# Four lasting two-bank PSUM buffers, used whole or by one bank, and a newly searched instruction order in a recurrence and FFN kernel

## The chip, the cores and the metric

The kernel runs on one NeuronCore of one Trainium2 chip. The metric is the device time of one execution in microseconds, from the median of the runs. The engines are TensorE (PE in the profile), VectorE (DVE), ScalarE (ACT), GpSimd (POOL) and SyncE (SP), which here only issues DMAs. PSUM, TensorE's output memory, has eight banks of 2 KB per partition.

## The reference

Two stages. First a linear-attention recurrence over 768 steps for 4 x 8 heads of width 40, then a feed-forward network on its 3072 rows of 320:

```python
for t in range(S):
    y[:, :, t] = np.einsum('bhd,bhde->bhe', rt, state)
    Sa = np.einsum('bhde,bhe->bhd', state, at)
    state_decay = state * wt[:, :, None, :] - np.einsum('bhd,bhe->bhde', Sa, bt)
    state = state_decay + np.einsum('bhd,bhe->bhde', vt, kt)
...
h = x @ w_in          # 320 -> 2048
r = np.maximum(h, 0.0)
return ((r * r) @ w_out).astype(np.float32)   # 2048 -> 320
```

Inputs and output are float32; the matmuls run on bfloat16.

## The kernel before, in words

**Chunks.** Time is cut into 12 chunks of 64 steps (c = 0 to 11). For each chunk the kernel loads r, k, v, w, a, b, prepares them (`prep`, `keys`, `keys_by8`), advances the state (`rec`), reads the result (`read`) and runs the feed-forward network on the chunk's 256 rows (`ffn`). Chunks 0 to 3 (BY8) use another layout of loads and keys than the later ones.

**The operations by name.** Each operation in the order has a short name with its chunk, and a suffix for its part:

- loads `ldw`, `ldk`, `ldb`, `lda`, `ldr`, `ldv` on SP; the weights come as `lwi`, `lwl`, `lwo`; the casts are `cast…`, `cwi`, `cwl`, `cwo`; the logarithms of the decays are `ln`, split into `hi` and `lo`
- sums of the decays on TensorE, `ci` and `cf`, and their exponentials on ScalarE: `eg`, `ef`, `ec`, `ei`, `ex` (lines 542, 603, 620, 626, 653)
- transposes on TensorE, `TA`, `TR`, `TK`, `TV`, `TU`, `TS`, `Tb`, `Tk`, `XT`, each followed by a copy or product out of PSUM under the same name with a small t. For the names in WIDE a transpose is done whole (128 x 128 blocks over the whole array, line 387), otherwise in pieces on half of the array (line 383)
- the two triangular products `EN` and `CX` in two halves g0 and g1, masked on VectorE by `mEN` and `mCX` (line 704)
- the recurrence: `AS`, `EV`, `u0`, `NU`, `u1` (VU), then `SC`, `S`, and `s`, which writes the state (line 796); the read-out is `RS`, `Y`, `y`, `yd`, `XT`, `xt`
- the first product of the network in four parts u0 to u3, each of eight matmuls `F` and four `FL` for the last 64 features on half of the array (line 893); then ReLU `f` (lines 921, 923) and square `q` (lines 927, 929, 931)
- the second product `O` in four parts (line 379): eight matmuls each, alternating between the two token halves, which lie in the two banks of one buffer. One copy `o` of 640 columns brings both halves out, one store `st` writes them. Only in the last chunk the halves are apart: `OL … g0` and `OL … g1` have a buffer each, of which one bank is used, and a copy `oe` each.

**The order.** Nothing is scheduled at run time or by the framework. A search outside the kernel wrote the text ORDER: entry after entry names the engine and the operation, and `Plan.issue` emits them in that order, so each engine's queue follows the text. A number behind PE is the PSUM buffer that the operation takes. Entries `W…` are filler matmuls that TensorE runs while it would wait (line 1044). Dependences between engines become semaphore waits when the program is built.

**PSUM.** There are four names pb0 to pb3, each two banks wide. Every operation that takes a buffer gets a new tile under that name (`slot`, and `fill` at line 1038), and waits until the readers of the one before are done.

Of the kernel before, what the change touches and what calls it, by code (L numbers as in the profile page):

```python
# [82 lines left out]
SP ldb 0; PE1 cf 0 h0; ACT castk 0; ACT ln 0 h1; SP lda 0; POOL castb 0; SP ldw 1; SP ldb 1; PE2 Tk
0; DVE hi 0 h1; DVE lo 0 h1; SP ldv 0; PE cf 0 h1; ACT eg 0; POOL castA 0; PE3 WD1; PE3 Tb 0; PE ci
0 h1; DVE tb 0 g0; SP ldk 1; ACT ef 0; ACT ln 1; SP ldr 0; SP lda 1; POOL hi 1; SP ldw 2; DVE tk 0
g0; ACT castb 1; PE1 WD3; PE1 TA 0; POOL lo 1; SP ldk 2; ACT ec 0; DVE tk 0 g1; DVE tb 0 g1; DVE tA
0 g0; DVE tA 0 g1; PE2 WD2; PE3 TU 0; ACT castV 0 g1; PE2 EN 0 g0; DVE mEN 0 g0; PE1 EN 0 g1; PE0
cf 1; POOL castV 0 g0; SP st0 0; POOL castk 1; DVE mEN 0 g1; PE2 ci 1; PE1 EV 0; ACT ec 1; DVE tU
0; PE2 Tb 1; DVE u0 0; PE3 Tk 1; ACT eg 1; PE NU 0; DVE tb 1 g0; POOL castR 0; POOL castA 1; SP ldv
1; ACT ef 1; DVE tb 1 g1; ACT u1 0 g0; SP lda 2; PE0 TR 0; SP ldr 1; ACT u1 0 g1; PE2 TA 1; ACT tR  # L90
0 g0; PE1 S 0 g0; DVE tk 1 g1; DVE tk 1 g0; DVE tA 1 g0; ACT tR 0 g1; PE S 0 g1; ACT ln 2; SP ldw
3; PE3 TV 0; DVE s 0 q1; PE0 EN 1 g0; DVE tA 1 g1; DVE s 0 q0; PE2 TU 1; DVE mEN 1 g0; ACT tV 0; SP
ldb 2; POOL hi 2; PE1 EN 1 g1; POOL lo 2; ACT castk 2; POOL castV 1 g0; DVE tU 1; SP ldv 2; PE3 cf
2; ACT eg 2; ACT ef 2; SP lwi 0 u1; PE0 CX 0 g1; PE2 AS 1; DVE mEN 1 g1; POOL castV 1 g1; PE EV 1;
PE1 CX 0 g0; ACT u0 1; POOL castA 2; PE3 ci 2; DVE mCX 0 g1; PE0 Tk 2; PE NU 1; DVE mCX 0 g0; ACT
ec 2; POOL castR 1; DVE tk 2 g1; DVE tk 2 g0; PE1 TA 2; PE3 TR 1; DVE tA 2 g0; PE0 SC 1; ACT u1 1
g0; POOL castb 2; SP ldk 3; POOL castV 2 g0; SP ldr 2; ACT u1 1 g1; PE2 Y 0; PE S 1 g0; DVE tA 2
g1; ACT ln 3; PE S 1 g1; PE1 TS 0; DVE y 0; DVE yd 0; ACT tR 1 g1; ACT tR 1 g0; DVE s 1 q0; SP ldw
4; SP lwi 0 u0; POOL hi 3; POOL castV 2 g1; DVE s 1 q1; PE2 Tb 2; DVE tb 2 g0; DVE tb 2 g1; PE3 TV
1; PE0 TS 1; PE2 TU 2; ACT tS 0; DVE tS 1; DVE lo 3; SP lwl 0; PE0 EN 2 g0; ACT tV 1; POOL cwi 0  # L100
u1; DVE mEN 2 g0; PE3 EN 2 g1; PE1 cf 3; DVE mEN 2 g1; PE0 CX 1 g1; ACT tU 2; POOL castk 3; PE2 AS
2; POOL castR 2; PE EV 2; PE3 CX 1 g0; ACT eg 3; ACT ef 3; PE1 XT 0; ACT u0 2; DVE mCX 1 g1; PE0 TR
2; PE NU 2; DVE mCX 1 g0; ACT tR 2 g0; PE3 ci 3; POOL cwi 0 u0; DVE xt 0; SP lwi 0 u2; ACT u1 2 g0;
ACT ec 3; PE1 F 0 u1; PE3 RS 1; PE Y 1; SP lwi 0 u3; ACT u1 2 g1; PE2 SC 2; DVE yd 1; PE S 2 g0;
POOL cwl 0; PE S 2 g1; DVE y 1; DVE s 2 q1; ACT tR 2 g1; ACT ln 4; PE3 XT 1; POOL cwi 0 u3; PE FL 0
u1; DVE xt 1; ACT f 0 u1; PE0 TV 2; DVE s 2 q0; ACT tV 2; PE3 Tk 3; PE1 F 1 u0; DVE tk 3 g1; DVE tk
3 g0; SP lda 3; PE2 TS 2; PE FL 1 u0; PE0 CX 2 g0; PE3 FL 0 u2; SP ldb 3; DVE tS 2; SP ldr 3; ACT
cwi 0 u2; DVE mCX 2 g0; PE F 0 u2; POOL hi 4; POOL lo 4; PE2 F 0 u3; SP lwo 0 x0; POOL castb 3; SP
ldv 3; SP lda 4; ACT castA 3; PE0 TA 3; SP lwo 0 x2; PE FL 0 u3; ACT f 1 u0; DVE f 0 u2; ACT f 0
u3; DVE tA 3 g0; POOL castR 3; PE1 FL 1 u2; DVE tA 3 g1; PE3 cf 4; PE F 1 u2; PE0 Tb 3; PE2 FL 1  # L110
u1; SP lwo 0 x1; DVE tb 3 g1; POOL castV 3 g0; ACT ef 4; ACT f 1 u2; POOL cwo 0 x0; POOL castV 3
g1; SP lwo 0 x3; ACT q 0 u2; PE3 CX 2 g1; PE F 1 u1; PE1 F 0 u0; ACT f 1 u1; PE FL 0 u0; DVE tb 3
g0; DVE mCX 2 g1; PE0 FL 1 u3; PE3 EN 3 g0; ACT f 0 u0; ACT q 0 u1; DVE mEN 3 g0; PE2 EN 3 g1; PE F
1 u3; POOL castA 4; SP lwo 0 x6; ACT f 1 u3; SP lwo 0 x5; DVE mEN 3 g1; ACT q 1 u0; PE1 TU 3; PE3
TR 3; PE2 AS 3; PE EV 3; POOL cwo 0 x1; PE0 ci 4 h1; DVE tU 3; DVE q 0 u0; ACT tR 3 g0; PE1 RS 2;
ACT u0 3; PE Y 2; PE NU 3; ACT ei 4 h1; DVE tR 3 g1; DVE y 2; DVE yd 2; ACT u1 3 g0; PE3 O 0 u0; SP
lwo 0 x4; PE1 SC 3; PE S 3 g0; SP lwo 0 x7; POOL q 1 u3; DVE u1 3 g1; PE S 3 g1; ACT ex 4 h1 g0;
DVE s 3 q0; SP ldw 5; PE2 ci 4 h0; DVE s 3 q1; ACT cwo 0 x2; ACT ex 4 h1 g1; POOL cwo 0 x3; SP ldb
4; POOL cwo 0 x6; PE0 XT 2; PE O 0 u1; ACT q 0 u3; SP ldk 4; ACT cwo 0 x4; PE1 TV 3; POOL cwo 0 x7;
ACT cwo 0 x5; ACT ex 4 h0 g1; ACT ei 4 h0; DVE xt 2; PE0 TA 4; PE O 0 u2; ACT ex 4 h0 g0; ACT ln 5;  # L120
PE O 0 u3; DVE tV 3; PE1 CX 3 g0; SP ldv 4; DVE tA 4 g0; DVE tA 4 g1; DVE hi 5; SP lda 5; POOL lo
5; PE0 TS 3; SP ldr 4; POOL mulKB 4 h0; POOL castV 4 g1; POOL castV 4 g0; ACT o 0; DVE mCX 3 g0; SP
lda 6; ACT q 1 u2; PE2 F 2 u0; POOL q 1 u1; PE FL 2 u0; PE1 FL 2 u1; PE F 2 u1; DVE tS 3; POOL
castR 4; ACT f 2 u0; PE0 FL 2 u3; PE2 CX 3 g1; DVE mulKB 4 h1; POOL castA 5; ACT f 2 u1; SP ldb 5;
PE3 ci 5 h1; ACT ei 5 h1; DVE mCX 3 g1; ACT ex 5 h1 g0; ACT ex 5 h1 g1; PE F 2 u3; PE1 TK 4; ACT f
2 u3; PE2 cf 5; ACT ef 5; DVE tK 4; PE3 F 2 u2; PE1 EN 4 g0; PE0 EN 4 g1; DVE mEN 4 g0; POOL q 2
u1; PE FL 2 u2; PE2 O 1 u0; DVE mEN 4 g1; PE1 RS 3; ACT f 2 u2; PE Y 3; PE3 AS 4; SP ldk 5; ACT q 2
u0; PE EV 4; PE O 1 u1; POOL q 2 u3; ACT q 2 u2; DVE yd 3; ACT u0 4; DVE y 3; SP ldw 6; PE1 ci 5
h0; PE0 XT 3; PE NU 4; PE O 1 u2; SP ldk 6; DVE u1 4 g0; PE O 1 u3; ACT ei 5 h0; ACT ex 5 h0 g1;
ACT u1 4 g1; DVE xt 3; PE3 TA 5; PE0 TR 4; ACT ex 5 h0 g0; POOL mulKB 5 h1; ACT o 1; ACT tR 4 g1;  # L130
SP ldr 5; DVE tA 5 g1; PE1 TV 4; PE2 SC 4; POOL mulKB 5 h0; PE S 4 g0; DVE tA 5 g0; PE S 4 g1; ACT
tR 4 g0; ACT ln 6; SP ldv 5; DVE tV 4; PE0 TK 5; DVE s 4 q1; PE3 FL 3 u3; PE F 3 u3; ACT tK 5; PE1
O 2 u0; DVE s 4 q0; ACT hi 6; ACT castR 5; PE0 CX 4 g0; PE2 CX 4 g1; POOL lo 6; SP ldb 6; PE O 2
u1; DVE mCX 4 g0; ACT f 3 u3; PE O 2 u2; ACT castV 5 g0; ACT q 3 u3; DVE mCX 4 g1; PE3 ci 6 h0; SP
st 0; ACT ei 6 h0; PE2 TS 4; PE0 EN 5 g1; ACT ex 6 h0 g0; PE O 2 u3; ACT ex 6 h0 g1; PE3 RS 4; DVE
tS 4; PE Y 4; PE2 EN 5 g0; DVE mEN 5 g1; PE0 cf 6; ACT o 2; PE1 ci 6 h1; DVE y 4; ACT ef 6; POOL
castV 5 g1; ACT ex 6 h1 g0; DVE yd 4; DVE mEN 5 g0; PE3 F 3 u2; PE0 F 3 u1; PE FL 3 u1; ACT ex 6 h1
g1; POOL castA 6; PE FL 3 u2; ACT ei 6 h1; DVE f 3 u1; PE1 XT 4; POOL mulKB 6 h0; PE2 AS 5; ACT f 3
# [942 lines left out]
```

## Time and profile before

| what | value |
|---|---|
| runs before | 243.8 and 244.61 us, median 244.21 |
| profiled execution, its own time | 242.46 us |
| its span, first to last instruction | 240.6 us |
| granted TensorE clock, mean | 0.997 |
| instructions on PE / DVE / ACT / POOL | 5526 / 227 / 228 / 126 |
| read from and written to HBM | 28.84 and 3.93 MB |

The span is the time from the first to the last instruction on the core; the rest of the execution's time lies around it. "Busy" is the time in which an engine has an instruction in work. Matmuls overlap in the array, so the mean length of one is longer than the distance between two; distances are read from groups in the chain and in the timeline. In the rows "pb" is a PSUM buffer, "x8" the number of instructions in the group, and a bracket at the end of a row is the idle time before it with what ended it.

### The profile page before, as it was taken

The page shows a single profiled execution, that of the slowest core. Times are in us where ns is not written, and L with a number is a line of the kernel's source. Part 1 is how long each engine was busy: PE and PEld are TensorE (multiplying, and loading weights), DVE is VectorE, ACT ScalarE, POOL GpSimd, SP SyncE. Part 2 cuts the span into 40 slices and gives each one's busy share as a digit, 9 for nine tenths or more (in the row PEclk, how much of TensorE's full clock was granted, in tenths as well). Part 3 has the DMA queues.
Part 4 walks back from the last instruction along what each step waited for, and adds up shares of the span by engine and source line. Part 5 has one row for each costly group of instructions (what it writes and reads, how often), then busy time and mean ns, then how long its engine had stood idle before and what let it go on. Part 6 is the DMA issues. An engine that isn't in the chain of part 4 may idle for free.

```text
span 240.6 us, 12143 instructions
## 1 busy us (share of the span) xinstructions
PE 223.9 (93%) x5526; PEld 175.8 (73%) x5526; DVE 179.6 (75%) x227; ACT 176.3 (73%) x228; POOL 125.1 (52%) x126
## 2 busy tenths in 40 slices
...
GB/s 99 208 232 180 225 169 207 277 248 177 315 120 174 187 115 172 224 183 158 173 172 151 177 178 178 131 44 126 161 116 6 4 3 23 94 3 3 57 0 108
DMA packets 100873, 33.55 MB, mean 139 GB/s; under 512 B 84950, under 2 KB 100822, under 8 KB 100822
## 3 DMA queue, kind: packets, MB, share of 16 engines
...
q8 instruction: 43, 0.70, 1.2%
...
HBM read 28.84 MB, written 3.93 MB: 136 GB/s over the span
## 4 chain that ended last, share of the span: by engine, by line
PE 68%; DVE 8%; issue 1%; ACT 1%; DVEq 0%
PE pb L379 36%; PE pb L893 23%; PE pb L383 7%; PE pb L387 2%; DVE STb L796 2%; DVE G L927 1%; DVE AR L679 1%; DVE VUT L360 1%; DVE EN L704 1%; DVE Yb L855 1%; DVE VU L362 1%; DVE CX L704 1%; ACT osb L365 0%; DVE KB L375 0%; ACT lnW L578 0%
## 5 line engine op out<-in xcount | busy, mean ns | idle before, releaser
L379 PE MATMUL pb<-WOUT,G 128*128 128x320 bf16 x384 | 56.8, 300 | 0.0
L929 POOL TENSOR_TENSOR G<-G 128x1024 bf16<-128x1024 bf16 x20 | 39.0, 1958 | 28.3 <-ACT G L921 28.1
L921 ACT ACTIVATE G<-pb 128x1024 bf16<-128x1024 f32 x40 | 40.6, 1022 | 15.4 <-PE pb L893 13.3
L893 PE MATMUL pb<-XT,WIN 128*128 128x256 bf16 x384 | 48.2, 273 | 0.5 <-issue 0.3
L379 PEld LDWEIGHTS <-G 128*128 128x128 bf16 x384 | 35.7, 98 | 14.2 <-issue 0.5
L893 PEld LDWEIGHTS <-WIN 128*128 128x128 bf16 x384 | 35.0, 98 | 8.4 <-issue 2.8
L373 POOL TENSOR_TENSOR KB<-raw_kb,iG 128x640 bf16<-128x640 f32 x14 | 21.7, 1552 | 31.7 <-ACT iG L620 23.7
L704 DVE TENSOR_TENSOR CX<-pb,MSKI 128x1024 bf16<-128x1024 f32 x24 | 28.7, 1218 | 5.8 <-PE pb L379 5.7
L704 DVE TENSOR_TENSOR EN<-pb,MSK 128x1024 bf16<-128x1024 f32 x24 | 28.7, 1217 | 3.8 <-PE pb L379 3.7
L931 ACT ACTIVATE G<-G 128x1024 bf16<-128x1024 bf16 x20 | 20.8, 1051 | 0.1
L796 DVE TENSOR_TENSOR STb<-pb,GT 40x640 bf16<-40x640 f32 x22 | 18.0, 820 | 2.3 <-PE pb L379 2.0
L373 POOL TENSOR_TENSOR lo<-lnW,hi 128x640 bf16<-128x640 f32 x10 | 14.0, 1399 | 9.7 <-ACT hi L365 5.0
L679 DVE TENSOR_TENSOR AR<-pb,GT 128x512 bf16<-128x512 bf16 x24 | 15.6, 684 | 3.2 <-PE pb L383 3.1
L893 PE MATMUL pb<-XT,WLAST 64*128 64x256 bf16 x192 | 17.5, 271 | 0.1
L379 PEld LDWEIGHTS <-EN 64*64 64x64 bf16 x768 | 14.2, 109 | 3.1 <-DVE EN L704 1.3
L923 DVE TENSOR_SCALAR G<-pb 128x1024 bf16<-128x1024 f32 x8 | 9.8, 1220 | 8.7 <-PE pb L893 8.6
L365 ACT ACTIVATE osb<-pb 128x640 f32<-128x640 f32 (+1 forms) x10 | 6.8, 677 | 12.3 <-PE pb L379 10.6
L855 DVE TENSOR_TENSOR Yb<-pb,Gin 128x640 bf16<-128x640 f32 (+1 forms) x24 | 12.4, 553 | 4.3 <-PE pb L379 4.2
L369 POOL CAST VU<-raw_v 64x640 bf16<-64x640 f32 x20 | 14.6, 734 | 1.3 <-DMA raw_v<-in_v_dram 0.7
L626 ACT ACTIVATE Gin<-pb 64x320 f32<-64x320 f32 x32 | 13.7, 428 | 1.5 <-PE pb L379 1.1
L653 ACT ACTIVATE GT<-pb 128x1024 f32<-128x1024 f32 x12 | 12.3, 1022 | 2.4 <-PE pb L379 1.9
L365 ACT ACTIVATE VU<-pb 64x640 bf16<-64x640 f32 x17 | 11.8, 696 | 2.9 <-DVE VU L362 1.6
...
## 6 DMA issues: line engine op xcount, KB each, us to landing
...
```

The lines of the kernel that those rows point to most:

```text
L365: alts.append(("ACT", c_act(n), lambda: nc.scalar.activation(out=o_(), in_=i_(), func=ACTF.Copy, scale=1.0 if scale is None else scale)))
L373: return [("POOL", 40 + 2.35 * n, lambda: nc.gpsimd.tensor_tensor(out=o_(), in0=a_(), in1=b_(), op=op)), ("DVE", c_dve(n), lambda: nc.vect ...
L379: return lambda: nc.tensor.matmul(out=o_(), lhsT=l_(), rhs=r_(), start=start, stop=stop, skip_group_check=True)
L383: return lambda: nc.tensor.transpose(out=o_(), in_=i_(), identity=IDb[64 * g:64 * g + n, 0:n])
L679: ew(f"tA {c} g{g}", [("DVE", c_dve(512), lambda g=g: nc.vector.tensor_tensor(out=steps(AR[q2][:, 0, g]), in0=turned(ha, g), in1=steps(GT[ ...
L704: ew(f"m{nm} {c} g{g}", [("DVE", c_dve(1024), lambda: nc.vector.tensor_tensor(out=dst[q2][:, g].rearrange("p q i t -> p (q i) t"), in0=slo ...
L796: ew(f"s {c} q{q}", [("DVE", c_dve(2 * n), lambda q=q: nc.vector.tensor_tensor(out=STb[q2][live(q), :, q, 0:D], in0=slot(hs, FP32)[live(q) ...
L855: return [("DVE", c_dve(2 * (f1 - f0)), lambda: nc.vector.tensor_tensor(out=Yb[q2][:, :, to:to + f1 - f0], in0=slot(hy, FP32)[:, :, f0:f1] ...
L893: return lambda: nc.tensor.matmul(out=o_(), lhsT=l_(), rhs=r_(), start=begins and opens(hf, x), stop=ends and not opens(hf, x), skip_group ...
L921: ("ACT", c_act(1024), lambda gb=gb, hf=hf: nc.scalar.activation(out=gb, in_=slot(hf, FP32)[:], func=ACTF.Relu)),
L929: ("POOL", 1900, lambda gv=gv: nc.gpsimd.tensor_tensor(out=gv, in0=gv, in1=gv, op=ALU.mult)),
L931: ("ACT", c_act(1024), lambda gv=gv: nc.scalar.activation(out=gv, in_=gv, func=ACTF.Square))],
```

## The change

- The four PSUM buffers are made once, at the start, and last for the whole kernel. A buffer is taken whole ("PE23": banks 2 and 3) or by one bank ("PE4": bank 4). Views of them replace the new tiles, and the flat views over both banks become views with a bank dimension (`block`, `by_head`, `turned`, `triangle`).
- The exponentials `eg` and `ef` of a chunk whose sums lie in the wide form (chunks 0 to 3) become two instructions, one for each bank (`exp_sums`).
- The second product is done by token halves in all chunks: `OL` in place of `O`, four matmuls an entry, one bank a half; two copies `oe` of 320 columns in place of one `o` of 640. The store stays one for both halves, except in the last chunk.
- The list WIDE: TA 3, 8, 11, TR 7, 8, 10, Tb 3, Tk 2 come in; TA 4, TR 3, TV 3, Tb 1, Tk 0 go out.
- ORDER is a new text from start to end: which engine takes which copy, in what sequence, which bank, and where fillers stand (24 whole and 8 half matmuls, before 6 whole).

```diff
-                self.fill(int(where[2:]), name[1], int(name[2:]))
+                self.fill([int(x) for x in where[2:]], name[1], int(name[2:]))
...
-                self.slot_of[h] = int(where[len(eng):])
+                self.slot_of[h] = sorted(int(x) for x in where[len(eng):])
...
+    PB = [ps.tile([128, 2, 512], FP32, name=f"pb{i}", tag=f"pb{i}", bufs=1) for i in range(4)]
     def slot(h, dt):
         if h not in slots:
-            i = plan.slot_of[h]
-            slots[h] = ps.tile([128, 2, 512 if dt == FP32 else 1024], dt, name=f"pb{i}",
-                               tag=f"pb{i}", bufs=1)
-        return slots[h]
+            slots[h] = pick_banks(plan.slot_of[h])
+        return slots[h] if dt == FP32 else slots[h].bitcast(dt)
+    def pick_banks(x):
+        return PB[x[0] // 2][:, x[0] % 2:x[-1] % 2 + 1, :]
...
+    def exp_sums(c, h, to, scale):
+        def go():
+            if wide_sums(c):
+                for x in range(2):
+                    nc.scalar.activation(
+                        out=to().rearrange("p (g b m) t -> p g b m t", g=2, b=2)[:, :, x],
+                        in_=slot(h, FP32)[:, x].rearrange("p (m g t) -> p g m t", g=2, t=L),
+                        func=ACTF.Exp, scale=scale)
+                return
...
-            if apart:
-                for g in range(2):
-                    pe(f"OL {c} u{u} g{g}", "D", DM, ms[g], reads=rd, writes=[ho + (g,)],
-                       alloc=[ho + (g,)] if u == 0 else [])
-            else:
-                pe(f"O {c} u{u}", "D", DM, [m for x in zip(*ms) for m in x], reads=rd,
-                   writes=[ho], alloc=[ho] if u == 0 else [])
+            for g in range(2):
+                pe(f"OL {c} u{u} g{g}", "D", DM, ms[g], reads=rd, writes=[ho + (g,)],
+                   alloc=[ho + (g,)] if u == 0 else [])
...
+        for g in range(2):
+            ew(f"oe {c} g{g}", copy_alts(lambda g=g: osb[q2][:, g, :], lambda g=g: bank(g), DM),
+               reads=[ho + (g,), ("left", c - 2)] + ([("osb", q2)] if c < 2 else []),
+               writes=[("osb", q2, g)], free=[ho + (g,)])
         if c < NCH - 1:
-            ew(f"o {c}", copy_alts(lambda: osb[q2][:], lambda: slot(ho, FP32)[:, :, 0:DM], 2 * DM),
-               reads=[ho], writes=[("osb", q2)], free=[ho])
```

The new order's entries of which the prediction speaks: its start, the second product of chunk 1, and its end:

```
SP ldw 0 h0; SP ldb 0; SP ldw 0 h1; POOL castb 0; ACT ln 0 h0; DVE hi 0 h0; SP ldk 0;
PE0 WD11; PE0 Tb 0; ACT ln 0 h1; DVE lo 0 h0; SP ldw 1; ACT castk 0; PE23 cf 0 h0; POOL hi 0 h1; SP
lda 0; SP lda 1; SP ldv 0; DVE lo 0 h1; PE1 WD1; PE cf 0 h1; PE1 WD5; PE45 ci 0 h0; SP ldk 1; ACT
eg 0; ACT ln 1; PE1 WD1; PE ci 0 h1; DVE tb 0 g1; DVE tb 0 g0; ACT castA 0; POOL hi 1; PE67 WR2;
PE67 Tk 0; SP ldb 1; ACT ef 0; DVE tk 0 g1; POOL lo 1; DVE tk 0 g0; ACT ec 0; PE01 TA 0; POOL castA
...
4; ACT ex 5 h0 g1; POOL q 2 u3; SP lda 6; ACT ex 5 h0 g0; DVE yd 3; ACT ei 5 h0; PE45 XT 3; PE67 TA
5; PE OL 1 u2 g0; POOL hi 6; SP ldw 7; ACT oe 1 g1; PE OL 1 u3 g0; ACT u1 4 g0; SP ldr 5; ACT u1 4
...
9; PE OL 10 u3 g1; PE OL 10 u3 g0; ACT oe 10 g0; POOL q 11 u2; DVE oe 10 g1; PE7 OL 11 u0 g0; PE OL
11 u2 g1; PE OL 11 u1 g0; SP st 10; PE OL 11 u3 g1; DVE oe 11 g1; PE OL 11 u2 g0; SP st0 11 g1; PE
OL 11 u3 g0; ACT oe 11 g0; ACT st1 11 g0; ACT st1 11 g1; SP st0 11 g0
```

More of the change, by code (lines that the diff above doesn't have):

```diff
@@ L83 @@
[L83 to L138, printed above, removed]
@@ new lines @@
+0; DVE mEN 2 g0; ACT castb 3; PE23 cf 3; SP ldr 3; ACT ef 3; ACT eg 3; PE67 AS 2; PE01 WR1; PE01 XT
+0; DVE xt 0; PE EV 2; SP lwi 0 u3; PE0 Tb 3; ACT castA 3; ACT u0 2; PE1 TR 2; PE23 CX 1 g1; DVE mCX
+1 g0; SP ldv 3; PE45 F 0 u1; ACT tR 2 g0; POOL cwi 0 u0; PE NU 2; SP lwo 0 x0; SP lwo 0 x2; DVE mCX
+1 g1; POOL cwi 0 u2; DVE tR 2 g1; ACT u1 2 g0; POOL castk 3; PE FL 0 u1; PE23 SC 2; SP lwo 0 x3;
+ACT u1 2 g1; PE1 TA 3; DVE tb 3 g0; PE S 2 g0; ACT f 0 u1; PE67 RS 1; DVE tA 3 g1; SP lwo 0 x1; DVE
@@ new lines @@
+POOL castV 5 g1; PE OL 2 u3 g0; SP ldr 7; ACT ex 6 h1 g0; ACT ex 6 h1 g1; PE45 RS 4; PE67 EN 5 g0;
+DVE oe 2 g0; POOL mulKB 6 h0; DVE mEN 5 g0; ACT ei 6 h1; POOL hi 7; SP ldw 8; PE01 TR 5; ACT castV
+5 g0; PE23 FL 3 u1; PE F 3 u1; ACT tR 5 g1; PE Y 4; SP ldv 7; ACT tR 5 g0; PE01 AS 5; DVE yd 4; PE
+EV 5; SP lda 7; ACT f 3 u1; DVE y 4; PE23 FL 3 u2; ACT u0 5; SP st 1; SP ldr 6; ACT q 3 u1; PE67 TA
+6; PE45 XT 4; DVE xt 4; PE NU 5; POOL lo 7; ACT u1 5 g0; PE F 3 u2; PE45 F 3 u0; POOL mulKB 6 h1;
```

254 lines of the change are left out of this document (150 added, 104 removed).

## The prediction

> **What bounds the kernel now.** I read the page's first part, then the busy times by stage, the chain, the groups by form, and the timelines of the head and the tail.
>
> ```profile
> span 240.6 us, 12143 instructions
> PE 223.9 (93%) x5526; PEld 175.8 (73%) x5526; DVE 179.6 (75%) x227; ACT 176.3 (73%) x228; POOL 125.1 (52%) x126
> ```
> ```profile
> core 0: us, PE busy (x) PEld busy (x) DVE busy (x) ACT busy (x) POOL busy (x), PEclk, DMA share, GB/s
> 0.00:54.00 54.00, 43.70 (x995) 35.23 (x996) 42.80 (x68) 38.55 (x47) 28.24 (x48) 1.00 0.87 205
> 54.00:227.00 173.00, 171.15 (x4468) 134.22 (x4467) 133.75 (x157) 134.30 (x178) 93.41 (x78) 1.00 0.61 126
> 227.00:240.60 13.60, 9.07 (x68) 6.36 (x65) 3.01 (x4) 3.48 (x5) 3.48 (x2) 0.95 0.18 48
> ```
>
> TensorE is the bound, but not everywhere alike. From 54 to 227 us it idles 1.85 us of 173, so an order can win almost nothing there; in the head it idles 10.3 us of 54, in the last stretch 4.5. In the head VectorE is as tight as TensorE:
>
> ```profile
> 20.00:30.00 10.00, 8.94 (x253) 7.40 (x254) 9.94 (x13) 8.59 (x12) 5.19 (x7) 1.00 0.91 208
> 30.00:40.00 10.00, 9.50 (x252) 8.35 (x250) 9.73 (x14) 8.27 (x9) 4.51 (x6) 1.00 0.78 184
> 140.00:180.00 40.00, 39.01 (x1112) 31.00 (x1114) 32.36 (x36) 31.43 (x42) 21.47 (x18) 1.00 0.66 133
> ```
>
> Busy TensorE time is not all streaming. The chain prices what lies between:
>
> ```profile
> 50.56 0.87 PE pb L893 x8
> 51.44 0.89 PE pb L387 x16
> ...
> 56.20 0.98 PE pb L893 x8
> 57.18 0.34 PE pb L383 x16
> ...
> 227.38 8.71 PE pb L379 x64
> ```
>
> Eight 256-column matmuls take 0.87 us when the next matmuls use the whole array too, and 0.98 when transposes on half arrays follow: changing how the array is divided costs 0.11. A whole transpose of 8 blocks takes 0.45 (0.89 for 16), a halved one of 16 pieces 0.23 (0.34 less the change). The second product takes 0.136 a matmul (8.71 over 64).
>
> **The change, part by part.** Counts are from the two written orders and the built programs.
>
> *TensorE's work.* The second product keeps its 384 matmuls; grouping them by token half instead of alternating costs nothing, because the last chunk was already grouped so and stands in the same 0.136. Whole transposes: TA goes from 3 to 5 chunks, TR from 4 to 6, TV from 4 to 3 (Tb and Tk only swap chunks): 4 x 0.22 for 8 blocks, less 0.43 for TV (0.89 against 0.46 for 32 halved pieces), is +0.4. Changes of the array's division, fillers left out, go from 185 to 197: 12 x 0.11 = +1.3. Together **+1.7 us**, nearly all of it behind 54 us, where nothing hides it.
>
> *The tail.* All two-bank buffers now last, and in the built program a wait on one bank also takes in the other bank of that buffer. OL 11 u2 g0 (bank 7) waits for VectorE's oe 11 g1, which reads bank 6; before, the last chunk's halves had buffers of their own and this wait wasn't there.
>
> ```profile
> 227.21 8.86 PE L379 MATMUL pb<-WOUT,G 128*128 128x320 bf16 x64
> 235.07 0.49 DVE L360 COPY osb<-pb 128x320 f32<-128x320 f32 x1 [0.86 <-PE pb L379]
> 236.11 0.44 ACT L365 ACTIVATE osb<-pb 128x320 f32<-128x320 f32 x1 [6.04 <-PE pb L379]
> 236.57 0.94 ACTq L973 DMA_DIRECT2D out_dram<-osb  x2
> ```
>
> The eight matmuls behind it (1.09 us, ending at 236.07 with their drain) began near 234.8, while that copy ended at 235.56. If they may start only then, the end moves by **+0.8**. What follows (copy 0.44, stores) is the same.
>
> *The same wait earlier.* The program has ten such waits on TensorE. Two more are bare: in chunks 1 and 2 ScalarE's oe g1 waits for OL u2 g0 (other bank), and OL u3 g0, TensorE's next instruction, waits for oe g1. Each costs the 0.44 copy and its hand-over both ways, which in the tail add up to about 0.25: **+1.4** for the two. Behind them stand the exponentials of the next chunk's sums on ScalarE and, on TensorE, all later work. One (a filler) is idle anyway, Tk 2 in the head is counted below, and the other five have 0.6 us or more of matmuls in front of them, which I take as cover; bare, they would cost 0.7 each.
>
> The Trainium skill, page "PSUM — Partial Sum Buffer", section "PSUM bank collisions raise a hardware error", says that two engines collide only in the same bank and quadrant, so the chip itself has no need of this wait. By that rule tail and pair would cost nothing and the sum be 2.2 less; the program waits nonetheless, since its semaphores, not the bank, hold TensorE.
>
> *VectorE, ScalarE, GpSimd.* The output copy is split everywhere: on ScalarE 2 x 0.44 for 0.70, on VectorE 2 x 0.49 for 0.82. The exponentials of chunks 0 to 3 become two each. Work also moves between engines.
>
> ```profile
> L923 DVE TENSOR_SCALAR G<-pb 128x1024 bf16<-128x1024 f32 x8 | 9.8, 1220 | 8.7 <-PE pb L893 8.6
> L927 DVE TENSOR_TENSOR G<-G 128x1024 bf16<-128x1024 bf16 x8 | 7.4, 930 | 0.0
> L362 DVE TENSOR_SCALAR VU<-pb 64x640 bf16<-64x640 f32 x7 | 5.7, 821 | 4.1 <-ACT iG L620 2.3 <-PE pb L379 1.4 <-ACT VU L365 0.3
> L375 DVE TENSOR_TENSOR KB<-raw_kb,iG 128x640 bf16<-128x640 f32 x2 | 2.6, 1317 | 0.0
> L365 ACT ACTIVATE osb<-pb 128x640 f32<-128x640 f32 x9 | 6.3, 704 | 6.3 <-PE pb L379 4.5 <-issue 1.1 <-DMA out_dram<-osb 0.7
> L360 DVE COPY osb<-pb 128x640 f32<-128x640 f32 x2 | 1.6, 824 | 4.7 <-PE pb L379 4.7
> L929 POOL TENSOR_TENSOR G<-G 128x1024 bf16<-128x1024 bf16 x20 | 39.0, 1958 | 28.3 <-ACT G L921 28.1
> ```
>
> VectorE gets 4 squares (3.7), 3 ReLUs (3.7), 4 u1 (3.3), 2 lo and 2 mulKB (5.2), ten half copies for two whole (3.3), a tV and a tS (2.0), and gives up 6.2: +15 us. ScalarE gets about +2.5; GpSimd loses about 14. Behind 54 us VectorE's share rises from 77% to about 87%, between the masks of chunk 4 and chunk 8 to 64.5 us against TensorE's 67.4 (before 51.8 against 61.7). It covers itself while TensorE has other work queued; if that cover goes, TensorE waits. Bounds: all 1.85 us of idle go (-1.85), or idle runs everywhere as in 140 to 180 us (0.99 in 40, 4.3 in 173: +2.4). I take the middle, **+0.3**.
>
> *The head.* I walked the new order with these durations.
>
> ```profile
> 4.18 0.43 POOL L259 TENSOR_SCALAR_AFFINE_SELECT UTI<-ones 64x64 bf16<-64x64 bf16 x2
> 7.98 0.35 POOL L325 MEMSET zero<- 4x320 f32 x1
> 10.07 1.02 ACT L542 ACTIVATE iG<-pb 128x1024 f32<-128x1024 f32 x1 [2.03 <-PE pb L379]
> 12.06 1.44 PE L1044 MATMUL pb<-UTI 128*128 128x512 bf16 x3
> 20.71 1.41 ACT L365 ACTIVATE VU<-pb 64x640 bf16<-64x640 f32 x2 [0.19 <-PE pb L379]
> 28.13 2.42 DVE L704 TENSOR_TENSOR CX<-pb,MSKI 128x1024 bf16<-128x1024 f32 x2
> 41.19 2.42 DVE L704 TENSOR_TENSOR CX<-pb,MSKI 128x1024 bf16<-128x1024 f32 x2
> 60.21 0.63 PE L379 MATMUL pb<-AR,KBT 64*128 64x64 bf16 x32
> 2.28 1.27 SPq L432 DMA_DIRECT2D raw_kb<-in_k_dram  x2
> ```
>
> Eleven fillers of about 0.4 (1.44 over three, cold) run from 4.6 to 9.1, beside the memsets that keep castb 0 until 8.4. SP issues a load in about 1.3 us; b 0 and w 1 go earlier, k 0 and a 0 by one or two places later. eg 0 ends near 12.2 (11.09 before): its sums come later and it is two instructions. u1 0 ends at 23.35 (22.12), because tU 0 and ef 1 now stand before u0 0 on ScalarE. The masks CX 0 end at 31.25 (30.55) and CX 1 at 46.4 (43.6); Tk 2 waiting for the other bank's tb 2 costs 0.5 to 0.7 of it. But chunk 3's transposes and products are drawn ahead: EN 3 starts at 54.4, not 60.2. By then the new order has done 35.1 us of TensorE work by my prices; the old one had done as much at 53.4. So **+1.0**, with bounds from -3 (most of the idle between first matmul and 54 us goes: 10.3 less the first 5.6, less what the first chunk must wait) to +3 (the lag of CX 1 stays).
>
> The Trainium skill, page "TensorE: Matmul & The Clock Gate", section "What's actually happening", says that the array runs at half clock until about 3.4 us of sustained work. The rows agree in kind: 0.4 us for a 512-column filler at 12 us. By the rule the eleven fillers have the array warm at the first transposes; if not, chunk 0's sums take 0.9 us longer and the sum is 0.9 more.
>
> *Sum:* 1.7 + 0.8 + 1.4 + 0.3 + 1.0 = +5.2. On the profiled execution's own 242.46 us (span 240.6) this is 247.7; the two other runs, 243.8 and 244.61, lie up to 2 us above it, and on their median it is 249.4. Between the two bases I forecast **248.0**, nearer to the profiled one, from which the terms are.
>
> **Rivals.**
> 1. *The head wins* (faster than before). Chunk 3's recurrence standing 6 us earlier lets the first product fill every wait. For it: the head is the only stretch with idle time. Against: VectorE is 97 to 99% busy from 20 to 40 us and gets no less work. Price: -4.7 in the head (all idle but the first 5.6), -1.8 behind it, +3.9 from work and waits: -2.6, 241.6 on the median. It decides if EN 3 starts before 52 us. Chance 0.22.
> 2. *VectorE becomes the bound* between chunks 4 and 8. For it: 64.5 us of work in TensorE's 67.4. Against: 102 us of VectorE's work in 111 of TensorE's over chunks 4 to 9 leaves slack. Price: +2.4 instead of +0.3, and the head's +3 instead of +1: 252. Chance 0.18.
> 3. *The one-bank use does not do what it says*, because waits take in the whole buffer. The five covered waits come bare, 3.5 more: 251.5. Against: the matmuls before them. Chance 0.08.
> 4. *The waits cost nothing*, as the PSUM rule would allow, and the head comes out even: +1.7 + 0.3 on the median, 246.2. Chance 0.12; the forecast itself 0.40.
>
> **How the numbers follow.** The forecast's own range is 245.5 to 250, rival 4 lies at its low end, the first rival at 240 to 244.2, the others at 249.5 to 253. A range of 241.5 to 252 leaves out under 2 in 10. About 2% (239.3 to 249.1) is what a measurement here tells from no change. Faster by more needs 4.9 us net, 8.8 with work and waits, of 10.3 idle: 0.05. Slower by more is rivals 2 and 3 and a small upper part of the forecast: 0.3. Within: 0.65.
>
> **What would show it.** TensorE's idle time from about 54 us to the last product near 2 us, and its work there 1 to 2 us longer; a gap of about 0.8 us before the last eight matmuls, and of 0.7 before the last four of the second product's half 0 in chunks 1 and 2; the first EN of chunk 3 near 54; VectorE near 194 us busy. A VectorE idle gap before masks together with TensorE gaps at 60 to 140 speaks for rival 2; EN 3 before 52 and a saturated TensorE from there, for rival 1.

## The result, and the profile after

The changed kernel takes 255.97 us (255.07 and 256.87) against 244.21. The ratio on record, over fast runs alone, is 1.0452 (95% interval 1.0394 to 1.051); the two medians give 1.0482. It is slower, 8 us above the forecast and 4 above the range. The first page and three stretches of the profiled execution (its own time is 255.07 us):

```profile
span 253.1 us, 12236 instructions
PE 230.4 (91%) x5536; PEld 178.2 (70%) x5536; DVE 194.0 (77%) x243; ACT 177.6 (70%) x244; POOL 113.2 (45%) x113
```
```profile
core 0: us, PE busy (x) PEld busy (x) DVE busy (x) ACT busy (x) POOL busy (x), PEclk, DMA share, GB/s
0.00:57.00 57.00, 46.91 (x1004) 36.99 (x1006) 42.99 (x69) 38.33 (x56) 27.13 (x45) 0.97 0.87 191
57.00:240.00 183.00, 175.17 (x4475) 135.58 (x4472) 146.70 (x171) 137.31 (x186) 84.05 (x67) 1.00 0.59 120
240.00:253.10 13.10, 8.37 (x61) 5.67 (x58) 4.31 (x5) 1.93 (x4) 1.97 (x1) 0.93 0.18 50
```

VectorE is busy for 194.0 us, as forecast. But from chunk 3's recurrence to the last products TensorE idles 7.8 us of 183, where it idled 1.85 of 173. So the middle, which I took for saturated, lost 6 us; the head ends later than forecast too. In the timeline of the changed kernel, EN of chunk 3 starts here (forecast 54.4, before 60.2):

```profile
57.26 0.52 PE L394 MATMUL pb<-AR,KBT 64*128 64x64 bf16 x24
```

Where the middle and the head stall, the rows of the same timeline name three kinds of cause. First the wait on the other bank, in chunk 1 where it was forecast (ScalarE's copy oe 1 g1, then OL 1 u3 g0, then SC 4; in chunk 2 the same gap is 0.53 us, at 107.90), in chunks 3 and 5 (OL 3 u0 g0, OL 5 u0 g0) where it was not, and in the tail (VectorE's oe 11 g1, then OL 11 u2 g0):

```profile
95.62 0.44 ACT L380 ACTIVATE osb<-pb 128x320 f32<-128x320 f32 x1 [1.50 <-PE pb L394]
95.95 1.40 ACT L380 ACTIVATE VU<-pb 64x640 bf16<-64x640 f32 x2
96.11 0.70 PE L394 MATMUL pb<-WOUT,G 128*128 128x320 bf16 x4 [0.53 <-ACT osb L380]
97.40 0.45 PE L394 MATMUL pb<-STb,IDQ 128*40 128x320 bf16 x4 [0.59 <-ACT VU L380]
...
122.12 0.74 ACT L380 ACTIVATE tA<-raw_a 128x640 bf16<-128x640 f32 x1
122.74 0.44 ACT L380 ACTIVATE osb<-pb 128x320 f32<-128x320 f32 x1
123.23 1.52 PE L394 MATMUL pb<-WOUT,G 128*128 128x320 bf16 x10 [0.66 <-ACT osb L380]
...
163.87 0.60 ACT L380 ACTIVATE AR<-pb 128x512 bf16<-128x512 bf16 x1 [1.85 <-PE pb L394]
164.52 0.70 PE L394 MATMUL pb<-WOUT,G 128*128 128x320 bf16 x4 [0.69 <-ACT AR L380]
...
247.16 0.49 DVE L375 COPY osb<-pb 128x320 f32<-128x320 f32 x1 [1.21 <-PE pb L394]
247.71 1.25 PE L394 MATMUL pb<-WOUT,G 128*128 128x320 bf16 x8 [0.58 <-DVE osb L375]
```

The brackets are the idle time and its releaser. Read the second pair: the copy oe 3 g1 reads bank 0, the product behind it writes bank 1; its matmuls in front were done in time, but on ScalarE the copy stood behind a logarithm and the cast at 122.12. In the third, ScalarE's tR 8 g1 reads bank 6 and waits 1.85 us for matmuls into bank 7.

Second, a VectorE operation of 3.2 us before TK 4 (the group at 81.15 is mulKB 4 h0, 0.82, and h1, 3.20):

```profile
80.48 2.06 POOL L384 CAST VU<-raw_v 64x640 bf16<-64x640 f32 x2
81.15 3.93 DVE L390 TENSOR_TENSOR KB<-raw_kb,iG 128x640 bf16<-128x640 f32 x2
82.51 1.88 POOL L951 TENSOR_TENSOR G<-G 128x1024 bf16<-128x1024 bf16 x1
85.14 0.52 PE L398 MATMUL pb<-IDb,KB 64*128 64x64 bf16 x24 [2.24 <-DVE KB L390]
```

It is the longest gap behind the head, and the prediction has no term for it.

Third, the head's hand-overs: tR 1 g1 waits for tA 2 g1 in the other bank, ec 2 stands behind it on ScalarE, TV 1 waits for ec 2, and s 1, behind tA 2 g0, holds EN 2 g1:

```profile
35.96 0.60 ACT L380 ACTIVATE AR<-pb 128x512 bf16<-128x512 bf16 x1 [0.51 <-DVE AR L701]
36.45 0.70 ACT L627 ACTIVATE Gin<-pb 128x640 f32<-128x640 f32 x1
36.59 0.69 DVE L701 TENSOR_TENSOR AR<-pb,GT 128x512 bf16<-128x512 bf16 x1 [0.66 <-ACT AR L380]
37.20 1.05 PE L402 MATMUL pb<-IDQ,VU 128*128 128x128 bf16 x16 [0.98 <-ACT Gin L627]
39.22 0.41 PE L394 MATMUL pb<-AR,KBT 64*128 64x64 bf16 x16 [0.96 <-DVE STb L818]
39.56 1.89 PE L402 MATMUL pb<-IDQ,STb 128*128 128x128 bf16 x16
```

The last row is slow by itself: the 16 transposes took 1.05 us in the row of 37.20, 1.89 here.

### The profile page after: what moved, and what is told of

It reads as the page before. It is cut to its first block, busy times and chain, and to the rows that moved or that the text cites. A ratio compares the mean times of both kernels' runs of the same rounds, so it can differ in the third digit from the quotient of the medians.

```text
span 253.1 us, 12236 instructions
## 1 busy us (share of the span) xinstructions
PE 230.4 (91%) x5536; PEld 178.2 (70%) x5536; DVE 194.0 (77%) x243; ACT 177.6 (70%) x244; POOL 113.2 (45%) x113
## 3 DMA queue, kind: packets, MB, share of 16 engines
HBM read 28.84 MB, written 3.93 MB: 129 GB/s over the span
## 4 chain that ended last, share of the span: by engine, by line
PE 71%; DVE 13%; ACT 8%; issue 5%; POOL 1%; DVEq 0%; ACTq 0%; POOLq 0%
PE pb L394 39%; PE pb L915 19%; PE pb L398 5%; PE pb L402 4%; PE pb L1059 3%; DVE KB L390 2%; DVE KBT L584 2%; DVE AR L701 2%; DVE CX L726 2%; ACT VU L380 1%; ACT osb L380 1%; DVE VU L377 1%; DVE STb L818 1%; DVE EN L726 1%; DVE osb L375 1%
## 5 line engine op out<-in xcount | busy, mean ns | idle before, releaser
L951 POOL TENSOR_TENSOR G<-G 128x1024 bf16<-128x1024 bf16 x18 | 34.5, 1920 | 43.3 <-ACT G L943 41.4
L394 PEld LDWEIGHTS <-G 128*128 128x128 bf16 x384 | 35.5, 98 | 17.8 <-issue 4.3
L943 ACT ACTIVATE G<-pb 128x1024 bf16<-128x1024 f32 x37 | 37.0, 1023 | 13.7 <-PE pb L915 13.2
L388 POOL TENSOR_TENSOR KB<-raw_kb,iG 128x640 bf16<-128x640 f32 x12 | 18.9, 1580 | 24.3 <-ACT iG L644 19.7
L953 ACT ACTIVATE G<-G 128x1024 bf16<-128x1024 bf16 x18 | 18.9, 1058 | 0.2
L380 ACT ACTIVATE AR<-pb 128x512 bf16<-128x512 bf16 x19 | 10.9, 598 | 8.0 <-PE pb L398 2.8
L945 DVE TENSOR_SCALAR G<-pb 128x1024 bf16<-128x1024 f32 x11 | 13.4, 1221 | 3.9 <-PE pb L915 3.7
L380 ACT ACTIVATE osb<-pb 128x320 f32<-128x320 f32 x13 | 5.7, 437 | 15.0 <-PE pb L394 14.1
L1059 PE MATMUL pb<-UTI 128*128 128x512 bf16 (+1 forms) x32 | 10.1, 456 | 5.7 <-POOL UTI L272 4.7
L388 POOL TENSOR_TENSOR lo<-lnW,hi 128x640 bf16<-128x640 f32 x8 | 11.2, 1401 | 8.4 <-issue 3.3
L877 DVE TENSOR_TENSOR Yb<-pb,Gin 128x128 bf16<-128x128 f32 (+1 forms) x24 | 12.4, 550 | 3.3 <-PE pb L394 3.3
```

The costliest lines, as they stand in the source:

```text
L380: alts.append(("ACT", c_act(n), lambda: nc.scalar.activation(out=o_(), in_=i_(), func=ACTF.Copy, scale=1.0 if scale is None else scale)))
L388: return [("POOL", 40 + 2.35 * n, lambda: nc.gpsimd.tensor_tensor(out=o_(), in0=a_(), in1=b_(), op=op)), ("DVE", c_dve(n), lambda: nc.vect ...
L394: return lambda: nc.tensor.matmul(out=o_(), lhsT=l_(), rhs=r_(), start=start, stop=stop, skip_group_check=True)
L943: ("ACT", c_act(1024), lambda gb=gb, hf=hf: nc.scalar.activation(out=gb, in_=slot(hf, FP32)[:], func=ACTF.Relu)),
L951: ("POOL", 1900, lambda gv=gv: nc.gpsimd.tensor_tensor(out=gv, in0=gv, in1=gv, op=ALU.mult)),
L953: ("ACT", c_act(1024), lambda gv=gv: nc.scalar.activation(out=gv, in_=gv, func=ACTF.Square))],
```

## The experiments

My theory after the result: the changed code is nearly free; the new order loses the time at a countable number of places, most of them waits on the other bank of a buffer. The rivals: the code costs it (split copies, lasting buffers), or VectorE, with 14 us more work, has become the bound, so that a wait taken out comes back elsewhere. All edits but the first change the written order alone; "ahead of" and "behind" are places in it. The diffs are cut down to the entries that move; others that stand between them are left out, not always with "...".

### The code in the old order

```diff
-PE3 O 0 u0 ... ACT o 0
+PE6 OL 0 u0 g0; PE7 OL 0 u0 g1 ... ACT oe 0 g0; ACT oe 0 g1
-PE3 EN 3 g0
+PE67 EN 3 g0
```

This cut is against the kernel before. Only the halves of the second product take one bank each. The list WIDE is the old one too.

> The changed code (lasting buffers, split copies and exponentials, second product by token halves) issued in the order of before, every buffer used whole. Theory (the new order lost the time, the code is nearly free): 244 to 247 us, within 1.5% of before, TensorE stalled and busy as before; the extra is some 0.2 us for each split copy and exponential on engines that have room. Rival (the code costs it: whole-tile waits, split copies, grouped matmuls): 252 to 257 us, near the changed kernel.

Measured: 244.16 us, 1.0007 times before (0.9961 to 1.0052). Lasting buffers, split copies, split exponentials and the second product by halves cost nothing that can be measured, used so and in the old order; by the interval, at most 1.3 us. So the loss comes with the new order, the one-bank use that it brings, and the new list WIDE, which this kernel takes back with it. What WIDE costs alone, no run shows.

### Three one-bank waits taken out

```diff
-ACT oe 1 g1; PE OL 1 u3 g0
+PE OL 1 u3 g0; ACT oe 1 g1
-ACT oe 2 g1; ... PE OL 2 u3 g0
+... PE OL 2 u3 g0; ACT oe 2 g1
-PE7 OL 11 u0 g0
+PE4 OL 11 u0 g0
```

> The changed kernel with the three bare one-bank waits taken out by order alone: the copies oe 1 g1 and oe 2 g1 are issued after the last matmuls of the other half, and OL 11 u0 g0 gets a buffer of its own (bank 4). Theory: the gaps of 0.70 and 0.75 before OL 1 u2 g0 and u3 g0, 0.70 before OL 2 u2 g0 and 0.75 before the last eight matmuls go, 2.0 to 2.9 us less, 253.1 to 254 on the median. Rival (VectorE and ScalarE bound these stretches): only the tail's 0.75 is won, what goes at chunks 1 and 2 comes back as a wait before chunk 3, 255.2.

Measured: 256.24 us, 1.0493 (1.0401 to 1.0585). The tail's gap went. In chunks 1 and 2 the gaps before u3 g0 went and came back at once, and larger: 1.82 us before SC 4 (0.53 and 0.59 before), and 1.25 at 109.55 for 0.53 in chunk 2. This is the timeline of that kernel; the first row is oe 1 g1, the second u1 4, the third SC 4:

```profile
95.25 0.44 ACT L382 ACTIVATE osb<-pb 128x320 f32<-128x320 f32 x1 [2.04 <-PE pb L396]
95.58 1.40 ACT L382 ACTIVATE VU<-pb 64x640 bf16<-64x640 f32 x2
97.03 0.45 PE L396 MATMUL pb<-STb,IDQ 128*40 128x320 bf16 x4 [1.82 <-ACT VU L382]
```

Nothing was won, nearly as the rival had it, but not because VectorE or ScalarE had too much work: ScalarE's copy now waits for the other half's matmuls, and the recurrence's u1 4 stands behind it in ScalarE's queue. I had moved the wait from one engine to another.

### The square beside VectorE's product

```diff
-POOL q 1 u2
...
 ACT f 2 u2
+ACT q 1 u2
```

> The changed kernel with the square of chunk 1 block 2 (q 1 u2) moved from GpSimd to ScalarE, behind its ReLU of chunk 2 block 2; it ran on GpSimd just while VectorE's mulKB 4 h1 took 3.20 us. Theory (GpSimd's access to SBUF holds VectorE's two-input operation): mulKB 4 h1 takes about 1.3 us, TensorE's gap before TK 4's end falls from 2.5 us to under 0.7, 254.0 us. Rival (VectorE's backlog before it is the cause): mulKB 4 h1 takes 3 us still, no gain or 1 us lost to ScalarE's extra square, 256 to 257.

Measured: 253.27 us, 1.0407 (1.0343 to 1.0471). The same rows as above, in this kernel:

```profile
82.33 2.07 DVE L392 TENSOR_TENSOR KB<-raw_kb,iG 128x640 bf16<-128x640 f32 x2
84.45 0.52 PE L400 MATMUL pb<-IDb,KB 64*128 64x64 bf16 x24 [0.38 <-DVE KB L392]
```

The two products take 2.07 us instead of 3.93, and TensorE's gap falls from 2.24 to 0.38. The local theory holds, 1.86 us as expected. How much of it reaches the end this run alone doesn't tell: against the unaltered kernel in a later run (below) the ratio falls by 0.006, and the two intervals overlap.

### Fillers in the head's gaps

```diff
+PE0 WD4
 PE01 TV 1
...
+PE2 WD3
 PE45 EN 2 g1
```

> The changed kernel with seven filler matmuls more, in the two idle gaps of TensorE around TV 1 (four before it, three before EN 2 g1), in buffers that are free there. Theory (the gaps of about 1 us each made the clock drop): granted clock 1.0 from 40 to 50 us, TS 1 and TU 2 at 1.05 us each instead of 1.9, EN 2 g0 1.5 us earlier, 254.5 us. Rival (the head hangs on ScalarE's and VectorE's chain): the clock is full but mEN 2 and tS 1 move by under 0.5, 255.5 to 256. Second rival: the clock drops anyway, for another reason.

The second fillers write over half of chunk 1's transposed r before it is read; this changes values, not the work. Measured: 256.85 us, 1.0595 (1.0503 to 1.0687). The clock was full and TS 1 took 1.05 us. But so it was in the next kernel, which has no such fillers and the gaps as they were. From 40 to 50 us, the profiled execution of the result and that of the control:

```profile
40.00:50.00 10.00, 9.83 (x220) 8.45 (x218) 7.23 (x8) 6.32 (x11) 5.66 (x6) 0.85 0.96 227
```
```profile
40.00:50.00 10.00, 9.67 (x256) 8.06 (x255) 7.96 (x9) 7.54 (x13) 5.43 (x6) 1.00 1.04 241
56.09 0.63 PE L396 MATMUL pb<-AR,KBT 64*128 64x64 bf16 x32
```

My theory of the clock falls: the same program, with the same gaps, has the drop in one execution and not in the other. It belongs to the execution shown in the result and costs it 1.2 us at EN 3 (57.26 against 56.09). The kernel before has runs with a mean granted clock of 0.985 to 1.000 too, so I don't count the drop to the change. The first four fillers had to wait for ec 2 as TV 1 does, and only pushed TV 1 back.

### The unaltered kernel, and the head mended

> The changed kernel itself, unaltered, so that the three others are read against it on the same chip: 254 to 257 us, 4.5% over before.

Measured: 255.68 us, 1.0469 (1.0429 to 1.0509). The three kernels after it ran on the same chip.

```diff
-DVE lo 0 h0; ... POOL hi 0 h1; ... DVE lo 0 h1
+DVE lo 0 h0; DVE hi 0 h1; DVE lo 0 h1
-PE0 Tb 0; ... PE23 cf 0 h0; PE1 WD1; PE cf 0 h1
+PE23 cf 0 h0; PE cf 0 h1; PE0 Tb 0
-DVE tA 2 g1; ... ACT tR 1 g1; ACT ec 2; DVE tA 2 g0; DVE s 1 q1; DVE yd 0; DVE s 1 q0
+DVE tA 2 g1; DVE tA 2 g0; ... ACT ec 2; ACT tR 1 g1; DVE s 1 q1; DVE s 1 q0; DVE yd 0
-PE4 Tb 2; PE NU 1; ... DVE tb 2 g1; ACT ef 2; PE5 Tk 2
+PE4 Tb 2; PE5 Tk 2; PE NU 1; ... DVE tb 2 g1; ACT ef 2
```

> The changed kernel with its head mended by order alone: hi and lo 0 h1 on VectorE straight after the first ones, Tb 0 behind the first sums, ec 2 ahead of tR 1 g1, tA 2 g0 straight after g1, Tk 2 beside Tb 2. Theory (the head's 4 us are hand-overs and one-bank waits on few places, not work): EN 0 at 15.3 instead of 16.3, TV 1 near 35.5 instead of 37.2, EN 3 near 54.5 instead of 57.3, and the time 2.5 to 3 us below the control. Rival (VectorE and the loads bound the head): EN 3 stays above 56.3, time 0 to 1 us below the control.

Measured: 253.62 us, 1.0374 (1.0332 to 1.0416), 2.1 us below the control, a little short of the 2.5 to 3 expected. EN 3 starts at 54.64, as the theory had it; TV 1 starts at 36.82 (37.30 in the control), not at 35.5. The first edits (hi, lo, Tb 0) did nothing; EN 0 was not earlier (16.71, control 16.41). The reason shows in the later kernel with all edits, which has them too:

```profile
12.54 1.29 DVE L585 TENSOR_TENSOR KBT<-pb,iG 128x512 bf16<-128x512 bf16 x2 [3.78 <-PE pb L1060]
```

Line 1060 is the filler's: tb 0 reads bank 0 and waits for fillers that TensorE writes into bank 1 of the same buffer, a whole microsecond after its operand was there (eg 0 ends at 10.45 + 1.09 = 11.54).

### All bare one-bank waits taken out

```diff
-ACT oe 1 g1; PE OL 1 u3 g0; ACT u1 4 g0; ACT u1 4 g1
+PE OL 1 u3 g0; ACT u1 4 g0; ACT u1 4 g1; ACT oe 1 g1
-ACT oe 2 g1; PE OL 2 u3 g0; ... ACT ei 6 h1
+PE OL 2 u3 g0; ... ACT ei 6 h1; ACT oe 2 g1
-ACT ln 8; ACT castA 7; PE OL 3 u3 g1; ... ACT oe 3 g1
+PE OL 3 u3 g1; ... ACT oe 3 g1; ACT ln 8; ACT castA 7
-DVE tR 8 g0; ... PE OL 5 u3 g1; ACT tR 8 g1
+ACT tR 8 g1; DVE tR 8 g0; ... PE OL 5 u3 g1
-DVE tA 11 g0; ACT oe 8 g0; ... DVE tA 11 g1; ... ACT castR 11; ACT f 9 u2
+DVE tA 11 g0; DVE tA 11 g1; ACT oe 8 g0; ... ACT f 9 u2; ACT castR 11
-DVE tA 8 g0; ACT tR 7 g0
+ACT tR 7 g0; DVE tA 8 g0
-PE7 OL 11 u0 g0
+PE4 OL 11 u0 g0
```

The last two edits of the kernel before (TA 2, TR 1, ec 2, Tk 2) are in it as well.

> The changed kernel with the bare waits on the other bank of a buffer taken out by order, at eight places: tail (bank 4 for OL 11 g0), oe 1 g1 behind u1 4 g1, oe 2 g1 behind ei 6 h1, oe 3 g1 ahead of ln 8, tR 8 g1 ahead of tR 8 g0, tA 11 g1 ahead of oe 8 g0, tR 7 g0 ahead of tA 8, and TR 1, TA 2, Tk 2 of the head. Theory (these waits are bare and add up): gaps before OL 1 u3 g0, SC 4, OL 2 u3 g0, OL 3 u0 g0, OL 5 u0 g0, CX 10 g1 and the last eight matmuls go, 4 to 5.5 us below the control, 250.5 to 252. Rival (VectorE bounds the middle): most comes back at the next VectorE result, as in the first try; 1 to 2 us below the control, of which the tail is 0.75.

Measured: 250.57 us, 1.026 (1.0212 to 1.0309): 5.1 us below the control, inside the theory's 4 to 5.5. Some 2.0 of it is the head's: TK 4 starts at 82.13, in the control at 84.14. Of the gaps expected to go, one stayed, 0.40 us before CX 10 g1. SC 4 with u1 4 ahead of the copy, then the page and the two stretches:

```profile
91.45 1.41 ACT L382 ACTIVATE VU<-pb 64x640 bf16<-64x640 f32 x2 [0.34 <-PE pb L396]
93.04 0.45 PE L396 MATMUL pb<-STb,IDQ 128*40 128x320 bf16 x4
93.15 0.44 ACT L382 ACTIVATE osb<-pb 128x320 f32<-128x320 f32 x1 [0.30 <-PE pb L396]
```
```profile
span 246.7 us, 12242 instructions
PE 228.8 (93%) x5536; PEld 176.8 (72%) x5536; DVE 193.6 (78%) x243; ACT 177.7 (72%) x244; POOL 112.7 (46%) x113
```
```profile
0.00:57.00 57.00, 48.18 (x1081) 37.64 (x1082) 45.41 (x72) 41.23 (x59) 28.85 (x48) 1.00 0.89 206
57.00:230.00 173.00, 168.07 (x4353) 130.05 (x4352) 140.82 (x165) 132.76 (x181) 81.91 (x65) 1.00 0.59 120
```

VectorE has the same 243 operations and 193.6 us of work, in a span 6.4 us shorter than in the result and 5.6 shorter than the control's 252.3. So VectorE's load did not bound the changed kernel; the waits were in its queue and the others'.

### All edits together

> Both of these edits and the square of chunk 1 block 2 on ScalarE together. Theory (few local causes, which add): 7.5 to 9 us below the control, 246.5 to 248.5, within 1.5% of before; what is left is the 1.7 us of TensorE's extra work. Rival (one bound, VectorE, behind all): 3 to 4.5 us below the control, 251 to 253.

Measured: 248.53 us, 1.0158 (1.0114 to 1.0202), 7.15 us below the control, just short of the 7.5 to 9 expected. The causes add within the noise: 5.1 for the kernel before this one, and 2.0 for the square and the first head edits, of which the latter won nothing above and the former 0.006 of the ratio, 1.5 us. Of the profiled executions, all with a granted clock of 0.997 or more, the control took 254.21 us, the last kernel 248.72 and this one 247.18.

### Five more

```diff
-PE1 WD5; PE45 ci 0 h0; ... PE1 WD1
+PE6 WD5; PE45 ci 0 h0; ... PE6 WD1
-PE4 WD2
-DVE mulKB 7 h1; ... DVE tS 5
+DVE tS 5; DVE mulKB 7 h1
-ACT ln 3; ACT hi 3; ... ACT ec 2
+ACT ec 2; ACT ln 3; ACT hi 3
-PE01 TS 3; PE67 F 2 u0
+PE67 F 2 u0; PE01 TS 3
-PE23 CX 10 g1; PE45 FL 9 u1
+PE45 FL 9 u1; PE23 CX 10 g1
```

> The kernel with all edits so far, and five more by the same reasoning: the fillers behind Tb 0 go to bank 6 instead of the other bank of Tb 0's buffer, the two fillers beside Tk 1 are dropped, ec 2 goes ahead of ln 3, tS 5 ahead of mulKB 7 h1, TS 3 behind F 2 u0, CX 10 g1 behind FL 9 u1. Theory (every bare wait that is taken out by order is won at the end): tb 0 g1 starts at 11.6 instead of 12.5, EN 3 near 53.5 instead of 54.6, 2 to 2.9 us less than with the edits so far, 245.5 to 246.5, within 1% of before. Rival (from here VectorE and the loads bound the head, so its waits only move): 0.8 to 1.3 us less, 247.2 to 247.8.

Measured: 245.97 us, on a chip on which before takes 243.04: 1.0135 (1.0082 to 1.0188). Against 1.0158 this is 0.6 us, nearer to the rival's figure; the two intervals overlap, so the gain is not sure. The starts moved as expected (EN 3 at 53.79, tb 0 now waits for its operand, row below), but TensorE's gap before TV 1 became one of 1.04 us before EN 2 g1, which waits for VectorE. From 20 to 45 us VectorE is busy for 23.34 of 25 us in this kernel, so it is probably the bound of the head once the needless waits are gone; no run tests that.

```profile
11.27 1.29 DVE L585 TENSOR_TENSOR KBT<-pb,iG 128x512 bf16<-128x512 bf16 x2 [1.78 <-ACT iG L527]
```
```profile
PE 228.0 (93%) x5533; PEld 176.8 (72%) x5533; DVE 192.7 (79%) x244; ACT 178.2 (73%) x245; POOL 108.8 (45%) x111
```
```profile
0.00:57.00 57.00, 47.74 (x1083) 37.77 (x1084) 46.84 (x74) 41.44 (x60) 26.60 (x45) 1.00 0.87 197
57.00:230.00 173.00, 170.37 (x4381) 132.05 (x4378) 139.95 (x165) 133.22 (x183) 80.23 (x65) 1.00 0.61 125
```

TensorE now idles 9.3 us of the head and 2.6 of 173 us behind it, about as before the change (10.3 and 1.85). What is left, some 3 us, stands in TensorE's own busy time, 228.0 us against 223.9, fillers among it.

### The fillers alone

The first three lines of the diff above, on the changed kernel.

> The changed kernel with its fillers alone altered: those behind Tb 0 in bank 6, the two beside Tk 1 dropped. Theory (a filler in the other bank of a buffer holds VectorE's copies like any one-bank wait): tb 0 g1 starts at 12.1, when eg 0 ends, instead of 12.57, tk 1 g0 at 22.1 instead of 22.7, and the head is 0.5 to 1.1 us shorter at EN 3; 254.6 to 255.2 against 255.7. Rival (the copies wait for other things there): no start moves by more than 0.2.

Measured: 255.26 us, 1.0525 (1.0468 to 1.0581), against 1.0469 for the unaltered kernel: no gain that can be told. The wait itself is gone: tb 0 starts when eg 0 has ended, at 11.46 + 1.08 = 12.54, and names it as its releaser. But eg 0 itself ends later here (12.10 in the control), so tb 0 starts no earlier than there (12.67), and the theory's 12.1 is not shown.

```profile
11.46 1.08 ACT L528 ACTIVATE iG<-pb 128x512 f32<-128x512 f32 x2 [2.23 <-PE pb L396]
12.58 0.69 DVE L586 TENSOR_TENSOR KBT<-pb,iG 128x512 bf16<-128x512 bf16 x1 [2.37 <-ACT iG L528]
```

What the edit wins is mostly lost on the way: TV 1 starts 0.5 us earlier than in the control (36.80 against 37.30), EN 3 0.14 (55.95 against 56.09), where 0.5 to 1.1 were expected. Starts behind 75 us are not compared, since the granted clock of this execution falls there (0.84 from 75 to 90 us).

### The converse: one buffer for the old order's last halves

```diff
-PE6 OL 11 u0 g0
+PE5 OL 11 u0 g0
```

> The changed code in the order of before, with one thing altered: the two halves of the last output, which had a buffer each there, take the two banks of one buffer. The converse of the wait's removal. Theory (the program waits for a buffer, not a bank): a gap of about 0.75 us appears before the last eight matmuls, and the time is 0.7 to 0.8 above the order of before, 244.9. Rival (the wait needs the new order's late copy): no gap, 244.2.

Measured: 243.61 us, 1.003 (0.9983 to 1.0077). The theory was wrong here. No gap opened on TensorE: in the old order the copy oe 11 g1 stands behind the last matmuls, so the copy waits. The last copies of the code in the old order, with two buffers, and with one:

```profile
235.87 0.49 DVE L376 COPY osb<-pb 128x320 f32<-128x320 f32 x1 [0.74 <-PE pb L395]
236.90 0.44 ACT L381 ACTIVATE osb<-pb 128x320 f32<-128x320 f32 x1 [6.04 <-PE pb L395]
```
```profile
235.81 0.44 ACT L381 ACTIVATE osb<-pb 128x320 f32<-128x320 f32 x1 [6.04 <-PE pb L395]
236.28 0.49 DVE L376 COPY osb<-pb 128x320 f32<-128x320 f32 x1 [2.23 <-ACT osb L381]
```

With one buffer the two copies also run one after the other, though they read different banks: the second starts 0.47 us after the first, though its matmuls were done before. Which instruction pays for sharing a buffer is set by their sequence in the order.

## Why the prediction was wrong, point by point

Three terms failed: the waits that it took as covered, VectorE's mulKB, for which it had no wait, and the size of the head.

- *TensorE's work, +1.7:* not tested by a run of its own. The last of the edits leave some 3 us, with TensorE busy for 4.1 us more than before, so 1.7 may be too little; the split between array changes, whole transposes and fillers stays open.
- *The tail, +0.8:* right. Idle 0.58 us, with the drain 0.75 (the last eight matmuls would otherwise follow at 0.54 us a four; they follow at 1.29). Taken out, it is gone. The rule of the Trainium skill, page "PSUM — Partial Sum Buffer", section "PSUM bank collisions raise a hardware error", lets two engines use different banks at once. By it the wait would have cost nothing, but the program's semaphores cover the whole buffer, and the 0.75 us were lost.
- *The same wait in chunks 1 and 2, +1.4:* right where it was put, too small in what hangs on it. Behind the copy on ScalarE I named the exponentials of later sums; the one that mattered was u1 4, for which SC 4 waited 0.59 us more.
- *"The other five have 0.6 us or more of matmuls in front of them, which I take as cover":* the step that failed among the waits. Matmuls in front cover TensorE only if the reader runs at once. The copy oe 3 g1 stood behind other work on ScalarE (0.66 bare), and the wait of OL 5 came by way of ScalarE's tR 8 g1 (0.69). Besides, I had counted waits on TensorE only. Those of VectorE and ScalarE on each other's bank (tR and tA in one buffer, a copy and tA 11) and on fillers come on top. Taking the bare waits out won 5.1 us, 2.0 of them in the head. Behind the head that leaves 3.1 (by the spans of the profiled executions 3.6), where tail and pair had been given 2.2; the two gaps taken as covered, 1.35 together, are about the difference.
- *VectorE, +0.3:* its load was right to the microsecond and did not bind; rival 2, at 252 the rival nearest to the measured time, had a cause that was not there. What I missed is one operation, and it is the largest single miss: I gave TensorE no wait for mulKB in particular, and it waits 2.24 us before TK 4. I priced mulKB from a row with a mean of 1317 ns, a mean of two (0.81 and 1.83), of which the longer, at 75.92, had run beside a product on GpSimd; unhindered it takes 0.82, beside GpSimd 3.20 here. The row carried the warning in it.
- *The head, +1.0:* wrong in size. EN 3 starts 1.7 us later than walked in the unaltered kernel's second profile (56.09 against 54.4), 2.9 later in the first, of which the clock's drop is 1.2. With only TA 2, TR 1, ec 2 and Tk 2 moved it starts at 54.24, so these hand-overs, two of them one-bank waits, are worth as much as it came late. The walk had priced Tk 2's alone.
- *The chances:* rival 3, that the covered waits come bare, was the right mechanism behind the head, and stood at 0.08. Its 251.5 is nearer to the result than it deserves: it priced five bare waits at 3.5, and two came bare at 1.35.
- *The size:* the control lies 11.5 us above the kernel before (255.68 against 244.2), and the sum was 5.2. Of the 6.3 us missing, the gap before TK 4 is 2.2, the head 1.7 and the waits taken as covered 1.35, an estimate from the gaps of the traces; about 1 us is not told apart. Another 1.4 us came from the base: on the median of 244.2 the sum gives 249.4, not 248.0.
